# Projections as pairs of half-height matmuls, and a layer norm finished on transposed tiles

## The chip, the core and the metric

The kernel runs on one core of a Trainium2 chip. A core has a matrix engine (TensorE, in the profile PE, with its weight loads as PEld), three engines for elementwise work (VectorE, in the profile DVE; ScalarE, ACT; GpSimd, POOL) and an engine that issues most DMAs (SyncE, SP). TensorE reads its operands from SBUF and writes sums into eight banks of PSUM. Each engine works through its own queue in order; they wait for each other on semaphores. The metric is the time of one execution in microseconds (us) on the device.

## The reference

One sequence of 2048 rows of 448 numbers, bf16, goes through two blocks: linear attention with softmax features, and a gated MLP whose gate mixes the rows. `c` gives a shift, a scale and a gate for each block.

```
mod = (silu(c) @ w_mod)            # six vectors of 448: sa, ca, ga, sb, cb, gb
h = layernorm(x) * (1 + ca) + sa
q, k, v = h @ wqkv                 # 16 heads of 28
pq, pk = q @ w_phi, k @ w_phi      # per head
phi(p) = concat(softmax(p), softmax(-p))
o = (phi_q @ (phi_k.T @ v)) / (phi_q @ sum(phi_k) + 1e-6)
x = x + ga * (o @ wo)
h = layernorm(x) * (1 + cb) + sb
z = gelu(h @ w_in);  z1, z2 = halves of 896
g = w_sp @ layernorm(z2) + b_sp    # 2048 x 2048, over the rows
x = x + gb * ((z1 * g) @ w_out)
```

## The kernel before

The 2048 rows are 16 tiles of 128 rows. `fast_path` allocates everything by hand and then runs through a long string, `ORDER`: each word is a step with its arguments, a PSUM slot after `@` and an engine after `/`. The order of the words is the order of the instructions in each engine's queue. A branch at the end repeats the whole in a general form, `general_path`, if a softmax sum grew too large; it isn't taken here.

The stages, by the names of the steps:

- Start. `ld:...` are loads. `ct`, `ce` make silu(c); `csA`, `ccA` (line 757, `colform`) multiply it with the shift and scale parts of `w_mod`, as columns. `FT`, `ET`, `PF`, `EP` fold `w_phi` into the q and k weights. `du` are matmuls on zeros that keep TensorE busy meanwhile.
- First layer norm. `l1s` (830) takes the moments of a tile, `l1r` (838) raises to the power -1/2, `l1a` (841) writes the normalised tile into `xpad`, four blocks of 112 columns, each padded to 128. `T1` (846, by DMA) or `X` with `XE` (854, by TensorE) transposes it into `hT`, four blocks of 112 rows.
- Scale and shift of the norm are put into the weights. `SH` (775) and `SHw` (780) multiply the weights by a tile that holds the shift, which gives the weights one more row, the shift's product; `SC` and `SCw` (784, 786) multiply the weight rows by 1 + scale. In `hT` a padding column of ones meets that row, so the first block has 113 rows.
- The k stage. `kM` and `vM` (864, 872) project one tile to k and to v, four matmuls of 112 or 113 rows each. `kE`, `kF` (867) take both exponentials, `kS` (878) sums them on VectorE, `kR` and `kP` divide, `kA` (895) adds a tile's product of features and values into a sum over all tiles, 8 matmuls of 116 columns. `KV` (901) takes the sum out.
- The q/n stage. `qM` (912) makes q transposed, in groups of 512 rows and two blocks; `qE`, `qF` (917) the exponentials. `nM` (940) gives the numerators and sums of one tile, 8 matmuls of 120 columns. `nX`, `nC`, `nS` (944 to 953) make the normaliser, `nT` (956) and `nA` (962) apply it. `T2` (846) transposes by DMA. `wM`, `wN` (972, 970) project with `wo`; `wN` adds x by an identity matmul. `wR` (977, 979) evicts, `wQ` (984, 986) squares, `l2R` (992 to 995) and `l2r` (998) make the moments, `l2a` (1001) normalises, `T3` (1006) transposes into `hT`.
- The z/y stage, interleaved with the end of the one before. `zM` (1012) makes the half of z that is normalised, 8 matmuls a tile, `zG` its gelu, `zQ`, `zR`, `zW`, `zN` (1036) its layer norm. `yM` (1042) makes the other half transposed, 28 groups of four matmuls, `yG` (1045) its gelu. `tT` (1086) makes differences of z2 blocks for the next stage.
- The spatial stage. `gM` (1058) and `pM` (1109) multiply with `w_sp`, in part by a scheme of seven block products, `sS` (1098) makes its sums of weights; `oM` (1071) projects with `w_out`, `oE` (1074) adds x, `oD` stores. `W` (1050) loads `w_sp` by transposing DMAs, all on SP.

## Time and profile before

| what | us |
|---|---|
| three runs, median (lowest, highest) | 258.0 (256.01, 258.09) |
| the profiled execution | 257.26 |
| its span, first to last instruction | 255.4 |
| busy in the span: TensorE, VectorE, ScalarE, GpSimd | 243.3, 193.9, 116.9, 98.1 |

The page of a profile sums each engine's busy time. The windows give it by stretches of the span. The chain of waits starts at the last instruction and goes back, at each step to what released it; the matmuls' spacing can be read there. The groups of instructions give one line for each source line, operation and shape, with the number, the busy time and the mean duration of one in ns; after the second bar stand the idle time of the engine just before them and what ended most of it. A matmul's duration there includes its way through the array, so it's longer than the spacing of two in a row. The timeline gives single instructions with their start and length. L864 is line 864 of the kernel before.

### The profile page before, as it was taken

Reading aid. Unit: us, or ns where it says so; the run is one execution under the profiler, and the core shown is the slowest. Engines: PE = TensorE matmul, PEld = TensorE weight load, DVE = VectorE, ACT = ScalarE, POOL = GpSimd, SP = SyncE. Lnnn points to the kernel's source line nnn. Section 1 sums busy time; section 2 is a strip of 40 time slices with the busy share of each in tenths; the row PEclk is TensorE's granted clock in tenths of the full one; section 3 lists DMA queues with packets and bytes.
Section 4 is the critical chain, followed back from the end, with each engine's and each line's share of the span. In section 5 each row is a group of like instructions: output and inputs, shape, how many; then the busy total and the mean of one; then the engine's idle time right before and its main releaser. Section 6 shows DMA issues by size and latency. Waiting matters only on the chain.

```text
span 255.4 us, 4195 instructions
## 1 busy us (share of the span) xinstructions
PE 243.3 (95%) x1501; PEld 127.2 (50%) x1509; DVE 193.9 (76%) x417; ACT 116.9 (46%) x244; POOL 98.1 (38%) x115
## 2 busy tenths in 40 slices
...
PEclk9999999999999999999999999999999999999999
...
GB/s 176 263 296 125 163 235 247 292 18 0 82 130 166 200 52 76 82 180 112 67 16 0 136 189 6 0 3 41 181 106 5 55 90 0 0 3 3 16 78 61
DMA packets 68655, 25.22 MB, mean 99 GB/s; under 512 B 58129, under 2 KB 68498, under 8 KB 68626
## 3 DMA queue, kind: packets, MB, share of 16 engines
...
q14 instruction: 15, 0.12, 0.1%
...
## 4 chain that ended last, share of the span: by engine, by line
PE 81%; DMA 5%; ACT 4%; DVE 4%; issue 2%; POOL 1%; SPq 1%; DVEq 0%; POOLq 0%; ACTq 0%
PE f_psum L1109 28%; PE f_psum L1071 8%; PE f_psum L1012 8%; PE f_psum L1042 7%; PE f_psum L1058 5%; PE f_psum L864 5%; PE f_psum L872 4%; PE f_psum L912 3%; DMA f_hT<-f_xpad 3%; PE f_psum L972 3%; PE f_psum L895 3%; DMA f_oo<-f_oo 2%; PE f_psum L726 2%; PE f_psum L940 1%; DVE f_t L956 1%
## 5 line engine op out<-in xcount | busy, mean ns | idle before, releaser
L1109 PEld LDWEIGHTS <-f_z2n 128*128 128x128 bf16 x192 | 18.7, 98 | 22.4
L1012 PE MATMUL f_psum<-f_win,f_hT 112*128 112x448 bf16 (+1 forms) x128 | 26.3, 352 | 1.0 <-DMA f_hT<-f_xpad 1.0
L1109 PE MATMUL f_psum<-f_wsp,f_z2n 128*128 128x512 bf16 x119 | 27.2, 379 | 0.1
L1042 PE MATMUL f_psum<-f_hT,f_win 113*128 113x512 bf16 (+1 forms) x112 | 26.1, 378 | 0.2 <-ACT f_z1T L1045 0.2
L1109 PE MATMUL f_psum<-f_hT,f_Eq 128*128 128x512 bf16 x92 | 22.3, 379 | 0.2
L1071 PE MATMUL f_psum<-f_wout,f_z1T 128*128 128x448 bf16 x112 | 21.7, 352 | 0.0
L1129 ACT COPY f_Eq<-f_psum 128x512 f32<-128x512 f32 x4 | 2.3, 586 | 41.0 <-PE f_psum L1109 41.0
L1012 PEld LDWEIGHTS <-f_hT 112*128 112x128 bf16 (+1 forms) x128 | 12.2, 97 | 13.3 <-DMA f_hT<-f_xpad 1.9
L1045 ACT ACTIVATE f_z1T<-f_psum 128x512 bf16<-128x512 f32 x28 | 16.0, 597 | 4.5 <-PE f_psum L1042 4.4
L878 DVE TENSOR_REDUCE f_ksum<-f_E 128x32 f32<-128x896 bf16 x16 | 16.8, 1067 | 1.0 <-ACT f_E L867 0.9
L917 ACT ACTIVATE f_Eq<-f_psum 112x1024 bf16<-112x1024 f32 x16 | 16.0, 1035 | 2.7 <-PE f_psum L912 2.7
L1042 PEld LDWEIGHTS <-f_win 113*128 113x128 bf16 (+1 forms) x112 | 10.7, 97 | 12.7 <-issue 0.4
L1016 ACT ACTIVATE f_z2g<-f_psum 128x896 bf16<-128x896 f32 x16 | 14.6, 914 | 4.9 <-PE f_psum L1012 3.9
L956 DVE TENSOR_TENSOR f_t<-f_psum,f_w 128x896 bf16<-128x896 f32 x16 | 16.7, 1084 | 0.2
L867 ACT ACTIVATE f_E<-f_psum 128x448 bf16<-128x448 f32 x32 | 15.4, 555 | 1.8 <-PE f_psum L864 0.9
L1071 PEld LDWEIGHTS <-f_z1T 128*128 128x128 bf16 x112 | 10.9, 98 | 10.0
L972 PE MATMUL f_psum<-f_win,f_oo 112*128 112x448 bf16 x64 | 14.4, 353 | 1.4 <-DMA f_oo<-f_oo 1.3
L1109 PEld LDWEIGHTS <-f_Eq 128*128 128x128 bf16 x96 | 9.4, 98 | 11.3 <-issue 0.2
L998 POOL TENSOR_TENSOR f_v<-f_v,f_mhalf 128x2 f32<-128x2 f32 x8 | 7.2, 904 | 20.3 <-DVE f_v L995 20.3
L912 PE MATMUL f_psum<-f_hT,f_Wq 113*128 113x512 bf16 (+1 forms) x64 | 14.9, 378 | 0.0
L998 POOL TENSOR_TENSOR f_zv<-f_zv,f_mhalf 128x2 f32<-128x2 f32 x8 | 5.7, 717 | 22.0 <-DVE f_zv L995 22.0
L1074 DVE TENSOR_TENSOR f_xpad<-f_psum,f_x 128x448 bf16<-128x448 f32 x16 | 9.8, 619 | 5.8 <-PE f_psum L1071 5.8
...
## 6 DMA issues: line engine op xcount, KB each, us to landing
...
```

The costliest lines, as they stand in the source:

```text
L867: nc.scalar.activation(out=Er[i % NR][:, s, :], in_=ps["k" + str(i)][:, 0, 0:D], func=ACT.Exp, scale=1.0 - 2.0 * s)
L878: nc.vector.tensor_reduce(out=ksum[:, i], in_=Er[i % NR][:].rearrange("p s (c f h) -> p (s c) h f", c=4, h=HP), axis=AX.X, op=ALU.add)
L912: nc.tensor.matmul(t[:, u, :], lhsT=Wq[0:KR[m], m, cc * CB:cc * CB + P], rhs=hT[0:KR[m], 4 * st:4 * st + 4, m, :], start=(m == 0), stop=(m ...
L917: nc.scalar.activation(out=Eq[st // 2][0:CB, 2 * c2:2 * c2 + 2, s, (st % 2) * 512:(st % 2 + 1) * 512], in_=ps["q" + str(n)][0:CB, :, :], f ...
L956: nc.vector.tensor_tensor(out=tr[i % 2][:], in0=numv(i)[:, :, :, 0:DH], in1=wr[i // 2 % 2][:, i % 2].unsqueeze(3).to_broadcast([P, 2, H, D ...
L972: nc.tensor.matmul(t[:, 0, 0:D], lhsT=oT[0:CB, i % 4, cc, :], rhs=wo_s[0:CB, cc, :], start=(cc == 0 and not with_x), stop=(cc == KC - 1))
L1012: nc.tensor.matmul(t[:, hf, 0:D], lhsT=hT[0:KR[m], i, m, :], rhs=win_s[0:KR[m], m, FH + hf * D:FH + (hf + 1) * D], start=(m == 0), stop=(m ...
L1016: nc.scalar.activation(out=stage_b()["z2g"][i % NZ][:], in_=ps["z" + str(i)][:, :, 0:D], func=ACT.Gelu_apprx_tanh, accum_out=zs1[:, i:i + 1])
L1042: nc.tensor.matmul(t[:, 0, :], lhsT=win_s[0:KR[m], m, fc * P:(fc + 1) * P], rhs=hT[0:KR[m], 4 * st:4 * st + 4, m, :], start=(m == 0), stop ...
L1045: nc.scalar.activation(out=stage_b()["z1T"][:, fc, st * 512:(st + 1) * 512], in_=ps["y%d_%d" % (st, fc)][:, 0, :], func=ACT.Gelu_apprx_tanh)
L1071: nc.tensor.matmul(ps["o" + str(t)][:, 0, 0:D], lhsT=later["z1T"][:, fc, t * P:(t + 1) * P], rhs=wout_s[:, fc, :], start=(fc == 0), stop=( ...
L1109: nc.tensor.matmul(t[:, 0, :], lhsT=b[:, j, f * P:(f + 1) * P], rhs=a[:, j, :], start=(PSTART[k] and j == 0), stop=(j == NH - 1), skip_gro ...
```

## The change

Rows and tiles. The 448 rows of a projection's contraction were four blocks of 112. Now they lie as seven halves of 64 in four blocks of 128 rows that begin at rows 0, 128, 192 and 320; rows 192 to 255 lie in two blocks. The weights are loaded in that form (`load_half`, two DMAs for one), `l1a` and `l2a` write the normalised tile in it (`lap`), with no padding.

```diff
+    HB = 64
+    OV = 192
+    ROWS = [0, P, OV, OV + P]
...
+    def load_half(eng, dst, src):
+        for a in range(2):
+            eng.dma_start(out=dst[:, 2 * a:2 * a + 2], in_=src[a * OV:a * OV + 2 * P].rearrange("(k p) n -> p k n", p=P))
...
+    def lap(v):
+        return bass.AP(v.tensor, v.offset, [list(v.ap[0]), [OV, 2], [1, 2 * P]])
```

Pairs. `rows_pair` computes two outputs u = 0 and 1, in two banks. In a first phase u = 0 takes the lower halves of the four blocks and u = 1 the upper halves, in turns. A second phase takes the other halves: three for each output, without the doubled one. Between the phases an empty instruction on TensorE waits for the last matmul of the first phase; `ORDER` says when the second phase comes, by a step with a `b` at its end (`zM:0 ... zMb:0`).

```diff
+    def rows_pair(key, outs, lhs, rhs, second_rows=((0, 2, 3), (0, 1, 3)), n=4, start=True, stop=True, flip=0):
+        def go(seq, first, last):
+            for k, (u, h, m) in enumerate(seq):
+                ins = nc.tensor.matmul(outs(u, m), lhsT=lhs(u, h, m), rhs=rhs(u, h, m), start=(first and k < 2),
+                                       stop=(last and k >= len(seq) - 2), skip_group_check=True)
+                yield ins
+
+        one = list(go([(u, u ^ flip, m) for m in range(n) for u in range(2)], start, False))
+
+        def two():
+            mark = nc.tensor.nop()
+            tc.add_manual_dep(mark.ins, one[-1].ins.name, mybir.DependencyInfo(mybir.DependencyClass.Sync, mybir.DependencyReason.DATA), reason="row halves")
+            list(go([(u, 1 - u ^ flip, m[u]) for m in zip(*second_rows) for u in range(2)], False, stop))
+
+        second[key] = two
...
     def zM(i, slot):
         t = ps["z" + str(i)] = bank(slot, "z2_ps")
-        for hf in range(2):
-            for m in range(KC):
-                nc.tensor.matmul(t[:, hf, 0:D], lhsT=hT[0:KR[m], i, m, :], rhs=win_s[0:KR[m], m, FH + hf * D:FH + (hf + 1) * D],
-                                 start=(m == 0), stop=(m == KC - 1))
+        rows_pair("zM%d" % i, lambda u, m: t[:, u, 0:D], lambda u, h, m: hT[half(h), i, m, :],
+                  lambda u, h, m: win_s[half(h), m, FH + u * D:FH + (u + 1) * D])
```

Two outputs are: k and v of a tile (`kv`, for `kM` and `vM`), the two blocks of a `qM`, the two halves of a `zM`, two blocks of a `yM` (14 pairs for 28). `kA`, `nM` and `wM` are written as pairs too, with all 8 halves for each output, since their rows aren't shared (128 or 112 rows a block); `wM` now takes two tiles at a time. `yG` evicts two banks at once.

Scale and shift. `SH`, `SHw`, `SC`, `SCw` and their tiles are gone. Scale and shift stand as columns in `ca1`, `sa1`, `cb1`, `sb1` and are applied to the transposed tile: in the eviction `XE` where TensorE transposes (tiles 0 to 7, four more than before), and in place by `h1` (tiles 8 to 15) and `h2` (all, for the second norm) where a DMA does.

```diff
+    def affine(eng, out_, in_, sc, sh):
         if eng is nc.scalar:
-            nc.scalar.activation(out=out_, in_=in_, func=ACT.Copy, scale=sc)
+            nc.scalar.activation(out=out_, in_=in_, func=ACT.Identity, scale=sc, bias=sh)
         else:
-            eng.tensor_scalar(out=out_, in0=in_, scalar1=sc, scalar2=None, op0=ALU.mult)
+            eng.tensor_scalar(out=out_, in0=in_, scalar1=sc, scalar2=sh, op0=ALU.mult, op1=ALU.add)
...
+    def hS(a, b, m, eng, sc, sh):
+        v = hT[:, a:b, m, :]
+        affine(eng, v, v, sc[:, m:m + 1], sh[:, m:m + 1])
```

Smaller edits. For 13 tiles `kS` becomes `kH` (GpSimd adds the two halves of the features) and `kG` (VectorE sums the rest); 3 keep `kS`. `nX` takes out both normaliser columns, `nC` is gone, `nS` is split into `nS`, `nV`, `nW`, some on GpSimd. `l2R` and `zR` may run on GpSimd, with one instruction more. `guard2` is split in two. The matmuls on zeros (`du`) shrink from 35 to 17.

`ORDER` is written anew. What the prediction speaks of: the branch `hint` comes first, the table load for gelu (`gt`) at the start; loads leave ScalarE's queue for SP's but for two; `T1` runs four times for six; five of eight `qM` come before `KV` instead of three; 9 of 16 `tT` and 11 instead of 2 `zN` go to GpSimd; 12 `wR` instead of 7 and 8 `wQ` instead of 3 go to VectorE; `h1` has 6 steps on VectorE and 2 on ScalarE, `h2` 12 on VectorE, 13 on ScalarE and 7 on GpSimd; `guard` moves from the spatial to the z/y stage. One line of each:

```diff
-zQ:0/S nM:10@A1 l2a:5/G nA:8/V zG:1 nM:11@A0 T3:4,6 yM:0,6@B0 nA:9/V nX:11 nX:10 zQ:1/S nC:11 zM:2@A2 nC:10 nS:5 T2:8,10 yG:0,6 zR:0,2 wQ:6/S
...
+nMb:12 T3:2,4 l2r:4,6 nV:5 T2:8,10 nW:5/V nX:12 nT:10 nS:6/G l2R:6,8/G nV:6 zM:0@A0 nA:10/V nT:11 zMb:0 nW:6/G l2r:6,8 nT:12 zM:1@A1 zG:0 l2a:4/G
```

The spatial stage's `gM`, `pM` and `oM` stay as they are.

347 lines of the change are left out of this document (175 added, 172 removed).

## The prediction

> **What bounds the kernel now.** I read the page first, then the windows cut at the stage borders, then the chain of waits, then the groups of instructions, and last the timeline where two engines meet.
>
> ```profile
> span 255.4 us, 4195 instructions
> ...
> PE 243.3 (95%) x1501; PEld 127.2 (50%) x1509; DVE 193.9 (76%) x417; ACT 116.9 (46%) x244; POOL 98.1 (38%) x115
> ...
> PEclk9999999999999999999999999999999999999999
> ```
>
> The profiled execution took 257.26 us, its span is 255.4; the median of the three runs, 258.0, is 0.3% above it. TensorE's clock is full throughout, so durations can be compared across the span. The windows cut the span at the first k matmul (18.4), at the end of the k/v sums (56.4), at the first `zM` (81.2), at the first `gM` (142.7) and at the last output add (250.9).
>
> ```profile
> core 0: us, PE busy (x) PEld busy (x) DVE busy (x) ACT busy (x) POOL busy (x), PEclk, DMA share, GB/s
> 0.00:18.40 18.40, 16.05 (x171) 11.87 (x172) 13.21 (x42) 10.36 (x19) 7.61 (x29) 1.00 0.98 244
> 18.40:56.40 38.00, 37.92 (x303) 22.27 (x302) 35.98 (x71) 30.22 (x58) 20.94 (x24) 1.00 0.89 187
> 56.40:81.20 24.80, 21.51 (x177) 12.12 (x175) 19.14 (x54) 20.77 (x41) 15.17 (x14) 1.00 0.53 89
> 81.20:142.70 61.50, 60.02 (x333) 29.95 (x334) 49.05 (x147) 51.28 (x121) 23.16 (x26) 1.00 0.44 88
> 142.70:250.90 108.20, 107.78 (x523) 50.96 (x529) 75.90 (x106) 4.23 (x8) 31.18 (x23) 1.00 0.26 53
> ```
>
> Columns after the length are busy times. In the k stage (second row) TensorE is full and VectorE nearly so (36.0 of 38.0); in the q/n stage (third row) nobody is full, a chain of latencies sets it; in the z/y stage (fourth) TensorE has 60.0 of 61.5; the spatial stage (fifth) is TensorE alone, and the diff leaves its matmuls as they are.
>
> What one matmul costs on the path is its spacing in the chain of waits (start, length, what):
>
> ```profile
> 22.63 2.28 PE f_psum L864 x12
> ...
> 40.02 0.42 PE f_psum L895 x8
> ...
> 143.32 6.64 PE f_psum L1058 x30
> ```
>
> ```profile
> 57.18 0.38 PE f_psum L761 x16
> 57.56 0.86 PE f_psum L940 x16
> 58.42 1.51 PE f_psum L780 x8
> 59.94 3.47 PE f_psum L912 x16
> ...
> 77.37 3.77 DMA f_hT<-f_xpad
> 81.14 0.05 issue
> 81.19 1.69 PE f_psum L1012 x8
> ```
>
> 448 columns: 2.28/12 = 0.190 us; 512 columns: 3.47/16 = 0.217; the 116 and 120 columns of `kA` and `nM`: 0.053; one column with its weight load: 0.38/16 = 0.024. So weight loads hide entirely behind 52 ns of streaming, and the number of passes through the array is what counts.
>
> **The change, part by part.** *Passes.* A projection over 448 rows now takes four matmuls of 112 rows per output. In the new `rows_pair` two outputs take 14 matmuls of 64 rows, two at a time on different halves of the array and into different banks: 7 passes instead of 8, if two halves take the time of one matmul. That saves 16 x 0.190 = 3.0 us on k/v, 8 x 0.217 = 1.7 on q, 3.0 on z and 14 x 0.217 = 3.0 on y: 10.8. `kA`, `nM` and `wM` keep their number of passes (8 pairs for 8 matmuls): 0. The shift matmuls `SH` and `SHw` go: 28 x 0.19 = 5.3. Four more tiles are transposed on TensorE (16 x 0.05 = 0.9). TensorE thus loses 15.2 us of path work, none of it in the spatial stage.
>
> The trace has no matmul of 64 rows. The nearest rows bound a pair from both sides: two serial matmuls are 2.0 of one; nothing but a hidden second load and issue is 1.0, since 2 x 0.024 = 0.048 us of load and issue still fits into the smallest pass, 0.053. Below 1.0 is excluded, because the columns still have to stream. I take 1.0: it lies by the row of single columns, and every load in this trace is hidden.
>
> *The wait in the middle.* Each pair group has a second phase that must not start before the first has landed in the banks, and an empty instruction on TensorE waits for it; all matmuls behind it in TensorE's queue wait too.
>
> ```profile
> L1012 PE MATMUL f_psum<-f_win,f_hT 112*128 112x448 bf16 (+1 forms) x128 | 26.3, 352 | 1.0 <-DMA f_hT<-f_xpad 1.0
> ...
> L972 PE MATMUL f_psum<-f_win,f_oo 112*128 112x448 bf16 x64 | 14.4, 353 | 1.4 <-DMA f_oo<-f_oo 1.3
> ```
>
> A matmul is over 352 - 190 = 162 ns after the next could start. In the new ORDER 15 of the 94 second phases follow their first phase with no TensorE work between, most others have 0.2 to 1.5 us between: 15 x 0.162 = 2.4 us, about 0.8 of it in the z/y stage. The order also passes 16 times between half-height and full-height matmuls, nearly all in the k stage. No row shows such a passage; bounds are 0 and one drain, 16 x 0.162 = 2.6, taken as the upper one, but in a stage where VectorE sets the pace. The Trainium skill, TensorEngine Tiling (Array Packing), section Key Properties, says that changing the tiling mode drains TensorE, which speaks against this change; by it the upper bound holds, and the total is 249 if TensorE should set the pace there, 246 if VectorE does.
>
> *z/y stage.* TensorE's 60.0 are 48.6 for z and y, 6 `nM` (2.5) and 10 output projections (8.6). Afterwards: 42.5, 2 `nM` (0.8) and 8 projections (6.1), together 49.4; the rest is moved ahead, into a stage where TensorE stands idle for 3.3 us and loses 4 x 4 shift matmuls (3.0) and two q groups. So what is late next are the other engines.
>
> ```profile
> L1036 DVE TENSOR_SCALAR f_z2n<-f_z2g,f_zm,f_zv 128x896 bf16<-128x896 bf16 x14 | 8.8, 663 | 3.0 <-POOL f_zv L998 2.9
> ...
> L885 POOL TENSOR_TENSOR f_phik<-f_E,f_kr 128x896 bf16<-128x896 bf16 x4 | 7.1, 1779 | 9.1 <-DVE f_kr L882 5.1 <-PE f_psum L864 3.3 <-ACT f_Eq L917 0.7
> ...
> L962 POOL TENSOR_TENSOR f_oo<-f_t 128x448 bf16<-128x448 bf16 x5 | 5.2, 1046 | 2.5 <-DVE f_t L956 2.4
> ...
> L1086 DVE TENSOR_TENSOR f_Eq<-f_z2n 128x768 bf16<-128x768 bf16 x4 | 3.0, 756 | 0.0
> ...
> L1036 POOL TENSOR_SCALAR f_z2n<-f_z2g,f_zm,f_zv 128x896 bf16<-128x896 bf16 x2 | 2.4, 1204 | 0.2
> ```
>
> Nine `zN` and nine `tT` pass from VectorE to GpSimd. VectorE loses 9 x 0.66 + 9 x 0.65 = 11.8 (0.65 is a middle of the four `tT` groups; the one shown is the longest); the other moves (more `wR` and `wQ` on it, `h2` new, `nC` and most of the moments gone) roughly cancel: 49 - 12 = 37. GpSimd gains 9 x 1.20 = 10.8 and nine `tT` of 768 elements, between the 448 of 1.05 and the 896 of 1.78, say 1.55: 14. So 23 + 25 = 48. ScalarE's 51.3 falls, since 28 `yG` become 14 of double width and 5 `wR` and 5 `wQ` leave it, while 13 `h2` come.
>
> Now the price of that cover. When both run, they slow each other:
>
> ```profile
> 134.59 0.55 DVE L1086 TENSOR_TENSOR f_z2n<-f_z2n 128x768 bf16<-128x768 bf16 x1
> ...
> 137.10 4.62 POOL L929 TENSOR_TENSOR f_wout<-f_wout,f_g_rep 128x448 bf16<-128x448 bf16 x4
> 137.17 2.35 DVE L1036 TENSOR_SCALAR f_z2n<-f_z2g,f_zm,f_zv 128x896 bf16<-128x896 bf16 x2 [0.82 <-POOL f_zv L998]
> 139.44 1.38 DVE L1086 TENSOR_TENSOR f_Eq<-f_z2n 128x768 bf16<-128x768 bf16 x1
> ```
>
> Alone a `tT` takes 0.55, beside GpSimd 1.38; two `zN` 2.35. With GpSimd busy nearly all the stage, VectorE's 5 `zN` (+0.5 each), 7 `tT` (+0.8) and some 17 short affine steps (+0.3) add 13: 37 + 13 = 50. TensorE 49, VectorE 50, GpSimd 48: no stage can be shorter than 50, and where the stage before stood 1.5 above its fullest engine, three equal ones will wait for each other more; I take 3.5. The stage: 61.5 to 53.5, **-8**.
>
> *q/n stage.* Its chain runs from `nM` over the normaliser, the transposes and the second layer norm to `zM`, with 3.77 us for one DMA transpose. The change takes the shift and scale of `win` out (cover, not path), adds one affine step `h2` on the transposed tile and joins two tiles per `wM` (one more tile's 0.76). Bounds -2 and +2; I take **-0.5**.
>
> *k stage and start.* The path to the first k matmul loses `SH` and twelve weight scalings; its new path needs both modulation loads, whose tile landed at 10.6 (row below), then a scaled eviction `XE`. That frees up to 5 us.
>
> ```profile
> 10.57 0.47 PEld L761 LDWEIGHTS <-f_wm 112*128 112x128 bf16 x16 [0.17 <-DMA f_wm<-in_w_mod_dram]
> ...
> 18.45 0.92 PE L864 MATMUL f_psum<-f_Wk,f_hT 113*128 113x448 bf16 x4
> ```
>
> ```profile
> L878 DVE TENSOR_REDUCE f_ksum<-f_E 128x32 f32<-128x896 bf16 x16 | 16.8, 1067 | 1.0 <-ACT f_E L867 0.9
> ...
> L841 DVE TENSOR_SCALAR f_xpad<-f_x,f_nm,f_rs 128x448 bf16<-128x448 bf16 x4 | 1.5, 366 | 0.0
> ...
> L732 ACT ACT_TABLE_LOAD x1 | 1.3, 1283 | 0.0
> ```
>
> But VectorE, with 49.2 in the first two windows, sets the pace. It saves 13 of 16 `kS` (13.9) and gets 13 `kG` over half the elements (0.55 each, bounds 0.53 and 1.07: +7.2), eight more `l1a` (+2.9) and some sixteen affine steps of about 0.3 (+4.8, replacing 5 scalings): about -2 net, while GpSimd's 13 new half sums of 448 elements (1.05 or more each) run beside it. Most of the earlier start is eaten: **-2.5**, bounds -6 and +2.
>
> *Queues.* Loads of k, v, q and the two `win` halves become two DMAs each with 512 rows for 448; on SP, which also takes three loads over from ScalarE's queue, 17 load issues become 25, in front of the spatial weights' transposes, which have 60 us to spare. 0.17 MB more at 244 GB/s is 0.7 us of a full first window, inside the bound. `T1` falls from six to four. Moving the Gelu table load to the start takes 1.3 us of ScalarE out of the q/n stage, or puts as much in if it has to be loaded again. The branch hint moved to the front and `guard` moved ahead lie beside idle engines: 0; a late branch would lengthen the 4.5 us behind the last add.
>
> The sum: -8 - 0.5 - 2.5 = -11, **257.3 - 11 = 246 us**.
>
> **The rivals.** *The halves overlap only in part* (slower). Let a pair take f of a matmul. For it: no row shows one; against it: no load is exposed. The z/y stage's 49.4 reach the old 60.0 at f = 1.21, the point from which it decides. At f = 1.3 they are 64, the stage 67 (+6), the k stage gains 35.6 x 0.3 = 10.7 us of TensorE work and ends 3 later: **266**. Chance 0.09. The Trainium skill, TensorE: Matmul & The Clock Gate, section Measured speedup vs the span model, gives four row tiles at 3.07 times one; an estimate from that is f = 4/3.07 = 1.30. No run here shows it yet.
>
> *The halves don't overlap at all*, so the change doesn't do what it says: all 102 us of paired passes twice, some 10 of it in idle time: **338**. Chance 0.04.
>
> *GpSimd becomes the bound.* If its operations stretch too beside VectorE, 48 us of it become 58, the stage is as long as before, and the rest nets to -2: **255 to 258**. Chance 0.14. Against it: the four gate products above kept 4.62/4 = 1.15 each while VectorE paid. For it:
>
> ```profile
> 191.28 1.15 POOL L1132 TENSOR_TENSOR f_junk<-f_Eq,f_bsp 128x512 f32<-128x512 f32 x1
> ...
> 192.33 1.22 DVE L1098 TENSOR_TENSOR f_hT<-f_hT,f_win 128x2048 bf16<-128x2048 bf16 x1
> 192.51 2.05 POOL L1133 TENSOR_TENSOR f_Eq<-f_Eq,f_bsp 128x512 f32<-128x512 f32 x1
> ```
>
> Here GpSimd pays, 2.05 for 1.15, and VectorE keeps its time.
>
> *TensorE stays the bound throughout* and all 15 come back, with an earlier start: below 237. Chance 0.05.
>
> **How the numbers follow.** The forecast, 237 to 255, has 0.68. One per cent of 258 is what a measurement can tell from no change, so faster means below 255.4: 0.68 + 0.05 + 0.02 of the GpSimd case = 0.75; within: 0.12; slower: 0.13. The range 237 to 258 leaves out the two overlap rivals and the largest gain, 0.18; its lower end is the stage sums at their favourable bounds (50 for z/y, -2 for q/n, -6 for k), its upper end the GpSimd case.
>
> **What would show it.** In the new profile: first and last starts of z and y matmuls, spaced 0.095 and 0.109 per half on average (right) or 0.19 and 0.22 (no overlap); the z/y window near 53 with TensorE near 50 and GpSimd above 45; VectorE's `tT` above 1 us; `zM` starting about 24 us after the sums; the spatial window still 108. It is wrong if the z/y window keeps its 61 us, or if the spatial window changes.

## The result, and the profile after

The changed kernel took 297.43 us (median of four runs, 295.65 to 298.46) where the kernel before took 257.78 beside it: 1.154 times as long, 95% interval 1.148 to 1.161. The prediction was 246, within 237 to 258. An execution more than 1.5% above the fastest of its kernel (one each of e5, e7 and e16, and one of the kernel before) counts in the medians below, but not in the ratios.

The page of the profile after, the lines that answer to the three of before:

```profile
span 293.8 us, 5440 instructions
...
PE 250.4 (85%) x2114; PEld 126.2 (43%) x2122; DVE 220.7 (75%) x393; ACT 114.4 (39%) x220; POOL 157.3 (54%) x192
...
PEclk9577998999867697799999999995999999999998
```

VectorE has 27 us more to do, not less, GpSimd 59 more, and TensorE's clock is no longer full: its mean over the span is 0.914. To see where the time went, I cut both spans at five marks: the first exponential of k (`kE`), the last pair of steps of `KV`, the first `zG`, the first `gM`, the last `oE`. All stage lengths below are between the starts of these steps, in profiled executions, one of each kernel.

| kernel | to first `kE` | k stage | q/n | z/y | spatial | last `oE` |
|---|---|---|---|---|---|---|
| before | 19.9 | 36.6 | 26.5 | 59.9 | 108.0 | 250.9 |
| after | 18.5 | 62.5 | 37.1 | 55.0 | 116.2 | 289.3 |
| difference | -1.4 | +25.9 | +10.6 | -4.9 | +8.2 | +38.4 |

Only the start and the z/y stage are shorter, the latter by less than forecast; the other three stages lose 44.7 us. The windows of the changed kernel between these marks (columns as in the windows of before), and then the first of the kernel before:

```profile
0.00:81.00 81.00, 60.41 (x723) 33.76 (x723) 63.31 (x129) 46.93 (x85) 45.60 (x59) 0.87 0.66 151
81.00:118.10 37.10, 28.81 (x370) 15.80 (x372) 27.48 (x62) 16.78 (x42) 20.15 (x44) 0.76 0.53 93
118.10:173.10 55.00, 51.23 (x503) 25.25 (x499) 42.41 (x102) 45.52 (x87) 46.12 (x64) 0.98 0.38 64
173.10:289.40 116.30, 109.97 (x523) 51.36 (x529) 86.93 (x102) 5.17 (x8) 45.46 (x28) 0.97 0.25 49
```

```profile
0.00:56.50 56.50, 54.07 (x473) 34.21 (x474) 49.26 (x113) 40.58 (x76) 28.64 (x53) 1.00 0.92 205
```

Up to `KV` VectorE works 63.31 us for 49.26 and is idle 17.7 for 7.2: of the 24.5 us by which that mark is later, 14.0 are more VectorE work and 10.5 more waiting.

**The work.** These groups of instructions of the changed kernel answer to the rows of `kS`, `kP`, `l1a`, `zN` and the gate products of before:

```profile
L1067 POOL TENSOR_SCALAR f_z2n<-f_z2g,f_zm,f_zv 128x896 bf16<-128x896 bf16 x11 | 13.6, 1244 | 0.4
...
L904 DVE TENSOR_REDUCE f_ksum<-f_hs 128x32 f32<-128x448 f32 x13 | 12.0, 932 | 3.9 <-POOL f_hs L901 3.9
...
L911 DVE TENSOR_TENSOR f_phik<-f_E,f_kr 128x896 bf16<-128x896 bf16 x9 | 9.5, 1054 | 0.6
...
L1137 DVE TENSOR_TENSOR f_hT<-f_Eq 128x2048 bf16<-128x2048 bf16 x4 | 8.0, 2026 | 0.0
...
L859 DVE TENSOR_SCALAR f_xpad<-f_x,f_nm,f_rs 128x512 bf16<-128x512 bf16 x12 | 6.2, 536 | 2.1 <-POOL f_rs L856 2.1
...
L948 DVE TENSOR_TENSOR f_wout<-f_wout,f_g_rep 128x448 bf16<-128x448 bf16 x5 | 5.8, 1215 | 0.0
...
L1067 DVE TENSOR_SCALAR f_z2n<-f_z2g,f_zm,f_zv 128x896 bf16<-128x896 bf16 x5 | 5.5, 1122 | 4.0 <-POOL f_zv L1031 4.0
```

A `kG` takes 932 ns over half the elements; the whole `kS` of before took 1067. So the 13 split sums save VectorE 13.9 - 12.0 = 1.9 us. And steps that the diff leaves as they are have become slower on VectorE, where GpSimd now runs much more beside it. `kP` and a sum of `sS` in the groups of the kernel before:

```profile
L885 DVE TENSOR_TENSOR f_phik<-f_E,f_kr 128x896 bf16<-128x896 bf16 x12 | 7.2, 625 | 0.1
...
L1098 DVE TENSOR_TENSOR f_hT<-f_Eq 128x2048 bf16<-128x2048 bf16 x4 | 5.2, 1290 | 0.0
```

So `kP` takes 1054 ns for 625, the sum 2026 for 1290, and `zN` 1122 for the 663 of the prediction's row. A gate product takes 1215; before, VectorE had one on `wout`, at 383, and one on `wo`, at 909, too few to say by how much it slowed. Single instructions point to GpSimd: in the kernel before most sums take 1.22 us while GpSimd is idle, and the two that start at 152.81 and 154.91, beside it, 2.18; in the changed kernel the `kP` at 59.90 takes 0.63 with GpSimd idle and the one at 70.67 1.97 beside a `kP` of GpSimd's. Not every step beside it pays: the `kP` at 42.53 keeps its 0.61.

**The waiting.** The chain of waits of the changed kernel shows one turn of its k stage, then the last steps ahead of `KV` (start, length, what):

```profile
49.00 7.29 PE f_psum L799 x85
...
57.37 1.04 POOL f_hs L901
58.43 0.96 DVE f_ksum L904
59.42 0.36 DVE f_kr L908
59.90 0.64 DVE f_phik L911
...
70.67 1.98 DVE f_phik L911
...
73.93 5.77 DVE f_wout L948 x5
```

Where a sum was one step on one engine, it now passes GpSimd and comes back. And five gate products, which have nothing to do with the k stage, stand on VectorE directly ahead of `KV`, for which the `nM` of the next stage wait. They take 5.77 us, of which about 2 hold `KV` up: the last `kA` ends at 77.5, and before that `KV` could not have begun. The 7.29 us of TensorE on the chain are the projections of late tiles in one lump, because their transposes came late. In the timeline SyncE's issues, then the last moments of tiles 8 to 11 on VectorE and their powers on GpSimd:

```profile
19.08 5.49 SPq L1089 DMA_TRANSPOSE f_wsp<-in_B_w_sp_dram  x3
38.54 10.35 SPq L864 DMA_TRANSPOSE f_hT<-f_xpad  x4
```

```profile
35.26 0.18 DVE L845 BATCH_NORM_AGGREGATE f_mv<-f_st 128x2 f32<-128x6 f32 x1
```

```profile
36.47 1.04 POOL L856 TENSOR_TENSOR f_rs<-f_rs,f_mhalf 128x4 f32<-128x4 f32 x1
```

SyncE issues nothing from 24.6 to 38.5, since `T1` of tiles 8 to 15 needs powers that GpSimd computes at 36.5 and 39.1. Two queues made them late: VectorE takes the last moments that the first of them needs at 35.3, behind its `kG`, `l1a` and `XE`, and a `kP` holds GpSimd until 35.9. In the kernel before the first `T1` is issued at 22.1 us.

### The profile page after: what moved, and what is told of

Its sections match the earlier page's. It is cut to its first block, busy times and chain, and to the rows that moved or that the text cites. A ratio compares the mean times of both kernels' runs of the same rounds, so it can differ in the third digit from the quotient of the medians.

```text
span 293.8 us, 5440 instructions
## 1 busy us (share of the span) xinstructions
PE 250.4 (85%) x2114; PEld 126.2 (43%) x2122; DVE 220.7 (75%) x393; ACT 114.4 (39%) x220; POOL 157.3 (54%) x192
## 4 chain that ended last, share of the span: by engine, by line
PE 45%; DVE 25%; POOL 13%; issue 7%; ACT 4%; DMA 4%; SPq 0%; DVEq 0%; POOLq 0%; ACTq 0%
PE f_psum L1148 21%; PE f_psum L799 13%; PE f_psum L1110 7%; DVE f_ksum L904 3%; POOL f_z2n L1067 3%; DMA f_hT<-f_xpad 3%; DVE f_hT L1137 3%; PE f_psum L1097 2%; DVE f_wout L948 2%; POOL f_zv L1031 2%; DVE f_phik L911 2%; DVE f_hT L785 2%; DVE f_Eq L1137 1%; POOL f_hs L901 1%; DMA f_x<-in_A_x_dram 1%
## 5 line engine op out<-in xcount | busy, mean ns | idle before, releaser
L799 PEld LDWEIGHTS <-f_hT 64*128 64x128 bf16 x448 | 22.2, 102 | 36.9 <-DVE f_hT L785 8.4
L799 PE MATMUL f_psum<-f_Wk,f_hT 64*128 64x448 bf16 x112 | 30.1, 403 | 5.5 <-DVE f_hT L785 3.0
L799 PE MATMUL f_psum<-f_win,f_hT 64*128 64x448 bf16 x224 | 27.5, 377 | 6.2 <-DMA f_hT<-f_xpad 2.6
L799 PE MATMUL f_psum<-f_wv,f_hT 64*128 64x448 bf16 x112 | 30.1, 403 | 0.0
L799 PE MATMUL f_psum<-f_hT,f_win 64*128 64x512 bf16 x196 | 23.4, 376 | 0.1
L901 POOL TENSOR_TENSOR f_hs<-f_E 128x448 f32<-128x448 bf16 x13 | 13.9, 1072 | 16.0 <-ACT f_E L891 10.7
L1148 PE MATMUL f_psum<-f_hT,f_Eq 128*128 128x512 bf16 x92 | 22.3, 379 | 0.2
L799 PE MATMUL f_psum<-f_win,f_oo 64*128 64x448 bf16 (+1 forms) x128 | 16.2, 376 | 3.1 <-DVE f_t L979 2.9
L799 PE MATMUL f_psum<-f_hT,f_Wq 64*128 64x512 bf16 x112 | 18.0, 453 | 0.1
L799 PE MATMUL f_psum<-f_vaug,f_phik 64*128 64x116 bf16 x256 | 12.5, 223 | 6.4 <-DVE f_phik L911 6.3
L1148 PE MATMUL f_psum<-f_Eq,f_oo 128*128 128x512 bf16 x47 | 13.0, 421 | 5.1 <-DVE f_z2g L1175 4.9
L1110 PEld LDWEIGHTS <-f_z1T 128*128 128x128 bf16 x112 | 10.9, 98 | 10.0
```

Of the source, the lines that this page charges most:

```text
L799: ins = nc.tensor.matmul(outs(u, m), lhsT=lhs(u, h, m), rhs=rhs(u, h, m), start=(first and k < 2), stop=(last and k >= len(seq) - 2), skip ...
L901: nc.gpsimd.tensor_tensor(out=hsum[i % 2][:], in0=ev[:, :, 0:DH // 2], in1=ev[:, :, DH // 2:DH], op=ALU.add)
L1110: nc.tensor.matmul(ps["o" + str(t)][:, 0, 0:D], lhsT=later["z1T"][:, fc, t * P:(t + 1) * P], rhs=wout_s[:, fc, :], start=(fc == 0), stop=( ...
L1148: nc.tensor.matmul(t[:, 0, :], lhsT=b[:, j, f * P:(f + 1) * P], rhs=a[:, j, :], start=(PSTART[k] and j == 0), stop=(j == NH - 1), skip_gro ...
```

## The experiments

Each kernel starts from the one named. All are judged beside runs of the kernel before on the same chip; "against after" gives the difference of the medians, and in brackets that of the ratios times 258 us.

| run | median | ratio to before (95%) | against after |
|---|---|---|---|
| e1 | 303.44 | 1.174 (1.170, 1.178) | +6.0 (+5.1) |
| e17 | 294.46 | 1.144 (1.136, 1.152) | -3.0 (-2.7) |
| e2 | 290.66 | 1.121 (1.117, 1.126) | -6.8 (-8.5) |
| e3 | 294.0, one execution | | -3.4 |
| e4 | 290.75 | 1.123 (1.117, 1.129) | -6.7 (-8.1) |
| e7 | 284.25 | 1.096 (1.091, 1.102) | -13.2 (-15.0) |
| e8 | 275.56 | 1.068 (1.060, 1.076) | -21.9 (-22.3) |
| e10 | 263.37 | 1.016 (1.010, 1.022) | -34.1 (-35.6) |
| e12 | 296.09 | 1.144 (1.137, 1.152) | -1.3 (-2.6) |
| e14 | 262.23 | 1.017 (1.011, 1.022) | |
| e15 | 258.86 | 1.004 (1.000, 1.007) | |
| e5 | 258.14 | 0.997 (0.993, 1.000) | |
| e6 | 269.06 | 1.040 (1.035, 1.045) | |
| e16 | 259.41 | 1.003 (0.999, 1.007) | |
| e9 | 259.66 | 1.007 (1.003, 1.011) | |
| e11 | 256.11 | 0.989 (0.987, 0.992) | |
| e18 | 258.48 | 1.001 (0.998, 1.003) | |
| e13 | 255.23 | 0.987 (0.984, 0.991) | |

### What are the halves worth?

**e1**: the changed kernel with its order, but each pair group as matmuls one after the other: for each output the blocks with all their rows, of the third block, which holds 64 rows twice, only the other 64.

```diff
+        proj = second_rows == ((0, 2, 3), (0, 1, 3))
+        for u in range(2):
+            for m in range(n):
+                h = 1 if proj and m == 2 else None
...
-            mark = nc.tensor.nop()
...
+            pass
```

> The changed kernel with every pair undone: the same ORDER, engines and row layout, but each output takes four full-height matmuls in one phase (128, 128, 64 and 128 rows for a projection), and nothing in the second. Theory A (the half-height pairs are good, and the time went to VectorE, GpSimd and the chains between them): TensorE's path work grows by about 11 us, most of it in its idle time, so 297 to 305 us, and no stage gets shorter by more than 2 us. Theory B (the pairs, their phase wait or the passage between heights cost the time): the k stage, 68 us now, falls by 10 us or more, and the time goes below 285.

**e5** and **e6** ask the same without the change's order. e5 is the kernel before up to `KV`, and behind it the second half of the change: `win` in halves, `h2`, pairs in `zM` and `yM`, in an order of my own. e6 is e5 with those pairs undone as in e1.

```diff
-    def SHw(n, slot):
...
+    def h2(a, b, m, eng):
+        hS(a, b, m, eng, cb1, sb1)
...
+        rows_pair("zM%d" % i, lambda u, m: t[:, u, 0:D], lambda u, h, m: hT[half(h), i, m, :],
+                  lambda u, h, m: win_s[half(h), m, FH + u * D:FH + (u + 1) * D])
```

> The kernel before with one half of the change alone: scale and shift of the second layer-norm on its transposed tiles (32 steps of 128x256 behind T3) and z and y as pairs of 64-row matmuls over seven halves; the projections of k, v, q, n and w, the first layer-norm, the single sums and the order up to the last k tile stay as before; the steps between KV and the spatial stage stand in an order of their own. Theory A (the halves are worth 6 us in the z/y stage and the 32 steps fit beside TensorE; the loss of the whole change is in its first half): 5 to 8 us under the kernel before, 250 to 253 us, from the first gelu of z to the first gM 52 to 55 us, k stage and spatial stage as before (36 and 108 us). Rival B (the 32 steps and the gelu pieces are a new bound on VectorE and ScalarE, so the second half gives nothing by itself either): 257 us or more.

> The kernel of e5 with its pairs undone: each unit of z and y in four matmuls (three of 128 rows, one of 64), everything else and the order the same. Theory A (TensorE bounds this stage, a pair costs one matmul): 16 x 2 x 0.19/2 us for z and 28 x 0.215/2 us for y, 6 us more than e5 where all of it is on the path, at least 4. Rival B (something else bounds it): within 1.5 us of e5. Rival C (the order alone is the gain): both e5 and e6 are under the kernel before by more than 4 us.

e6 is 10.9 us slower than e5, more than the 6 us of passes that the pairs of z and y save. e1 is 6.0 slower than the change; its z/y stage is 11.7 longer, but its spatial stage, against its expectation, 6.0 shorter. The z/y window of e6 says that TensorE is full, and its chain of waits why:

```profile
87.10:154.30 67.20, 66.63 (x289) 22.20 (x290) 54.13 (x145) 48.08 (x92) 40.73 (x44) 1.00 0.47 83
```

```profile
93.85 0.97 PE f_psum L828 x4
94.82 0.76 PE f_psum L1010 x4
```

Four matmuls of one `zM` output take 0.97 us, four of a `wM` 0.76. The undone form passes from 128 rows to 64 and back in each output, and that costs 0.21. So these two runs compared the halves with something slower than what there was before. **e16** takes the passages out of e6, **e17** out of e1 for z and y alone (its k, v and q keep them), and **e18** is e11 (below) in the form of e16: all four blocks with 128 rows, so that 64 rows count twice and z is another z.

```diff
-                h = 1 if proj and m == 2 else None
+                h = None
```

> e6 with one thing changed: the third block of each z and y projection is also taken with all 128 rows, so that no 64-row matmul stands among the 128-row ones any more. The number of matmuls stays (four for an output); the 64 rows that lie in two blocks are counted twice, so z is another z. In the chain of waits of e6 a wM of four 112-row matmuls takes 0.76 us, eight zM matmuls (two outputs) take 1.93 to 2.01 and sixteen yM matmuls 4.08, where four times 0.190 and 0.217 would give 1.52 and 3.47. Theory A: each passage between 128 and 64 rows, two for an output, costs some 0.08 to 0.10 us of TensorE; e6 holds 60 outputs and so about 11 us of it, and the 10.9 us between e6 and e5 priced more than the halves. Then eight zM matmuls take 1.52, TensorE in the z/y stage falls from 66.6 to 56, the stage from 67.2 to 58, the time to 259 to 262, and the halves are worth 1 to 4 us. Theory B: the matmuls are slow for another reason (128 rows instead of 112, the rows' place), and nothing changes: eight zM matmuls still 1.9 to 2.0, 267.5 to 270.5 us.

> e1 with the same change for zM and yM alone: their third block with all 128 rows, the rows that lie in two blocks counted twice; k, v and q as in e1. Theory A (a passage between 128 and 64 rows costs 0.08 to 0.10 us): the z/y stage falls from 66.7 to 57 to 59, the spatial stage gets some of the 6 us back that it had won, the time is 296 to 300. Theory B (no price on the passage): 302 to 305, z/y stage 66 to 67.

> e11, the fastest kernel so far, with its pairs undone as in e16: four matmuls of 128 rows for each output of z and y, the 64 rows that lie in two blocks counted twice, so z is another z. In e11 the z/y stage takes 53.4 us with TensorE busy 51.85; eight matmuls for seven are 32 x 0.095 + 28 x 0.109 = 6.1 us more of TensorE. Theory A (TensorE bounds the stage; the halves are worth what they save): z/y 58 to 60, 260 to 263 us. Theory B (as in e16, where TensorE had 54.9 of 58.0 and the time was 1.3 above e5: the chain through GpSimd and the transposes bounds the stage as much, and the pairs pay for passages and for the wait in their middle): z/y 54 to 56, 256 to 258.5 us, the halves are worth 0 to 2.5.

The z/y window of e16:

```profile
84.90:144.20 59.30, 55.79 (x291) 26.89 (x291) 51.97 (x138) 47.28 (x92) 42.27 (x45) 1.00 0.56 94
```

TensorE has 10.8 us less than in e6 with as many matmuls: 60 outputs with two passages each, 0.09 us a passage. Theory A of the passages held for e16, and e17 went even below its range: with full height in z and y and the order of the change the time is 294.5 us, with halves 297.4; the intervals of the ratios overlap, so that the halves are worth nothing there that can be measured. In the better orders they are worth 1.3 us by the medians and 1.7 by the ratios, whose intervals just touch (e16 against e5), and 2.4 or 2.9 (e18 against e11, by theory B of that run: TensorE isn't the only bound).

This isn't for want of overlap. TensorE's timeline in the changed kernel, at full clock:

```profile
60.81 0.35 PE L799 MATMUL f_psum<-f_wv,f_hT 64*128 64x448 bf16 x1
60.81 0.35 PE L799 MATMUL f_psum<-f_Wk,f_hT 64*128 64x448 bf16 x1
```

```profile
163.64 2.83 PE L799 MATMUL f_psum<-f_win,f_hT 64*128 64x448 bf16 x28
166.29 6.87 PE L799 MATMUL f_psum<-f_hT,f_win 64*128 64x512 bf16 x62
```

Two halves start together, and 14 pairs take 166.29 - 163.64 = 2.65 us, 0.189 each, the time of one full matmul: f = 1.0, and the rivals that rested on f are out. What the empty instruction costs can be read too, where a second phase follows its first at once:

```profile
121.58 1.73 PE L799 MATMUL f_psum<-f_win,f_hT 64*128 64x448 bf16 x14
123.14 1.92 PE L799 MATMUL f_psum<-f_hT,f_win 64*128 64x512 bf16 x14
```

The seven pairs of one `zM` take 123.14 - 121.58 = 1.56 us where 7 x 0.189 is 1.32: 0.24 for the wait between the phases. In the row of 14 pairs, two tiles whose phases take turns, there is none.

That the halves gain nothing is for want of a stage that TensorE alone bounds. The chain of waits of the changed kernel from 118 to 175 us, summed by line:

```profile
by line: POOL f_z2n L1067 16.3%; issue 12.8%; POOL f_zv L1031 9.7%; PE f_psum L799 7.1%; DVE f_xpad L1034 5.7%; POOL f_v L1031 4.3%; DVE f_z2n L1067 3.9%; POOL f_z2n L1125 3.5%; POOL f_oo L1125 2.9%; DVE f_x L1008 2.9%; POOL f_Eq L1125 2.8%
```

It runs through GpSimd's `zN`, powers and `tT`; matmuls have 7% of it. With full height (e17) TensorE is busy 54.41 of 55.7 us, with halves 51.23 of 55.0: less work for TensorE only uncovers that chain. Both are near to full, and taking the steps off GpSimd (e4, below) shortens the stage by no more than 1.9.

**e9** and **e11** are e5 in two other orders behind `KV`, since e5 had lost in the q/n stage (32.9 us for 26.5) what it gained in z/y (55.1 for 59.9). Its timeline, and the window in which that begins:

```profile
64.12 1.78 PE L973 MATMUL f_psum<-f_KVbd,f_Eq 112*128 112x120 bf16 x16 [2.17 <-DVE f_t L989]
```

```profile
64.00:68.00 4.00, 3.88 (x37) 2.76 (x38) 3.26 (x10) 0.37 (x2) 1.03 (x1) 0.51 0.34 64
```

TensorE waits 2.17 us for VectorE, and the granted clock (third number from the end) is then 0.51, in the next 4 us 0.63. That a wait is paid twice in this way is not a rule: e16, in the same order, waits as long at the same place,

```profile
64.61 1.01 PE L978 MATMUL f_psum<-f_KVbd,f_Eq 112*128 112x120 bf16 x16 [2.16 <-DVE f_t L994]
```

and its clock stays at 1.00. Its q/n stage takes 28.6 us, so that some 4 of the 6 us that e5's profiled execution lost there went with the clock.

```diff
-h2:0,1,0/V nS:5 ld:win0/Y nA:8/G
+l2a:2/G wQ:4/S ld:win0/Y h2:0,1,0/S T2:6,8
```

```diff
-l2a:2/G wQ:4/S ld:win0/Y h2:0,1,0/S T2:6,8
+kP:15/V gr:0@A1 ld:win0/Y kA:15@A0 KV:1
```

> The second half of the change alone, as e5, in an order whose stretch from KV to the first z leaves TensorE no wait above 1.2 us (in e5 a wait of 2.17 us ended at 64.12 us and the granted clock was 0.51 in the 4 us after it). Theory A (e5 lost to that wait what its z/y stage of 55.1 us had won against 59.9): q/n stage 27 to 29 us (e5 32.9, before 26.5), z/y 53 to 56, 251 to 254 us. Rival B (the steps of scale and shift lengthen the way to the first z by themselves): q/n again 31 us or more, 257 us or more.

> The second half of the change alone, as e5 and e9, in an order that also keeps the loads of win ahead of the transposes T2 that it would hold up (in e9 a T2 issued at 81.68 us, 1.2 us behind the load of win0, held TensorE for 3.21 us). Theory A (the halves and the 32 steps are a gain of 4 us or more once the stretch from KV to the first z has no such wait): q/n 27 to 29 us, z/y 53 to 55, 251 to 254 us. Rival B (the stretch to the first z is longer by the steps themselves): q/n 31 us or more and 256 us or more.

e9 has no such wait at that place, and its clock is full there, but by its numbers it came out as rival B (q/n stage 32.3 us). It lost 3.2 us at a place that the timeline shows, SyncE's first and then TensorE's:

```profile
80.44 1.08 SPq L663 DMA_DIRECT2D f_win<-in_B_w_in_dram  x2
81.68 1.24 SPq L879 DMA_TRANSPOSE f_oo<-f_oo  x1
```

```profile
87.44 1.69 PE L1005 MATMUL f_psum<-f_win,f_oo 112*128 112x448 bf16 x8 [3.21 <-DMA f_oo<-f_oo]
```

The transpose `T2` is issued behind two loads of `win` (448 KB each) and lands 5.7 us later; the median of its kind in that run is 3.1. In e11 that load stands ahead of `KV`. e11 is the fastest kernel of this study with the whole computation, 1.1% faster than the kernel before (interval 0.8 to 1.3); and as e18, its twin at full height, is at 1.001, the gain is that of the halves. It missed the time of theory A too and meets both conditions of rival B. That the steps `h2` are the reason, as B says, isn't shown: without them (e13) the stage still takes 31.1 us. Its q/n stage, 32.5 us, is nearly full on VectorE from 64 to 89 us, as one window out of it shows,

```profile
68.00:72.00 4.00, 2.80 (x30) 1.82 (x28) 3.90 (x7) 2.51 (x7) 2.94 (x3) 1.00 0.16 33
```

and in its z/y stage TensorE's timeline has the passages again, as e11 keeps its output projections `wM` at full height:

```profile
111.42 0.93 PE L1005 MATMUL f_psum<-f_win,f_oo 112*128 112x448 bf16 x4
112.29 1.69 PE L818 MATMUL f_psum<-f_hT,f_win 64*128 64x512 bf16 x14
113.90 0.93 PE L1005 MATMUL f_psum<-f_win,f_oo 112*128 112x448 bf16 x4
```

The four `wM` matmuls take 112.29 - 111.42 = 0.87 us where 4 x 0.190 is 0.76, the seven pairs 1.61 where 7 x 0.217 is 1.52: 0.1 a passage. The change writes `kA`, `nM` and `wM` as pairs too, though that saves no pass; it saves passages.

### Do scale and shift on the tiles cost?

**e13** is e11 without its 36 `h2`; **e14** is e10 (below) without its 12 `h1`, **e15** without those and its 32 `h2`.

```diff
-h2:0,1,0/V nS:5 ld:win0/Y
+nS:5 ld:win0/Y
```

> The kernel of e11 without its 32 steps h2: scale and shift of the second layer-norm are left out of the result, everything else stands as it was. Theory A (the steps behind T3 are the price that the second half pays: they lie between each transpose and its z, and their 15 us of engine time lie on engines that are busy): 3 to 6 us under e11, from KV to the first z 2 to 4 us shorter. Rival B (they are hidden; the stretch from KV to the first z is set by VectorE's steps on the numerators): within 1.5 us of e11.

> The kernel of e10 without its 12 steps h1: scale and shift of the first layer-norm are left out for tiles 4 to 15, everything else the same. Theory A (of the 10 us that the k stage of e10 is longer than before's 36.6, these steps in the path of the transposed tiles are a third or more): k stage 43.5 us or less, 3 us or more under e10. Rival B (they are hidden, the k stage is set by what stands in VectorE's and ScalarE's queues: moments, sums, exponentials): within 1.5 us of e10.

> The kernel of e10 without h1 (tiles 4 to 15) and without the 32 steps h2, both left out of the result. Theory A (the steps of scale and shift on tiles are what the change pays with): e10 less what e14 and e13 give together, at least 6 us, so 257 us or less, under the kernel before. Rival B: less than 3 us under e10.

Leaving out `h2` in e11 gives 0.9 us (0.5 by the ratios), leaving out `h1` in e10 1.1, which by the ratios is nothing, so both runs went by rival B; both left out of e10 give 4.5 by the medians and 3.3 by the ratios. So `h2` is nearly covered in e11, and `h1` in e10; in e10 the two together are worth some 3 us. `h2` alone was not left out of e10.

### What does the order cost?

**e2**: `kS` for all tiles, no `kH` and `kG`. **e3**: the half sums in bf16 instead of f32. **e4**: `tT`, `zN`, the moments' steps and `h2` from GpSimd to VectorE, the order kept.

```diff
-kH:0 kE:1 kv:2@A1 l1s:8 W:0,2 kH:1 kv:3@C kG:1
+kE:1 kv:2@A1 l1s:8 W:0,2 kv:3@C kS:1/V
```

```diff
-    hsum = [aph.tile([P, 8, DH // 2, HP], F32, name=f"f_hs{r}") for r in range(2)]
+    hsum = [aph.tile([P, 8, DH // 2, HP], BF, name=f"f_hs{r}") for r in range(2)]
```

```diff
-zN:1/G
+zN:1/V
...
-tT:1,0,2/G
+tT:1,0,2/V
...
-zR:0,2/G
+zR:0,2/V
```

> The changed kernel with the feature sums of all 16 tiles in one VectorE step again (kS for kH and kG). VectorE's step goes from 0.93 to 1.07 us, 13 x 0.14 = 1.8 us more, and GpSimd loses 13.9 us and a link of the chain from exponential to division. Theory A1 (the split is one of the main losses): the k stage, 68 us, falls by 5 us or more, time 285 to 293. Theory A2 (it is only VectorE's amount of work): the k stage grows by about 2 us, 297 to 300. Theory B: no change.

> The changed kernel with the half sums kept in bf16, which rounds them once more. If VectorE's sum over them (0.93 us for 448 numbers in f32, against 1.07 for 896 in bf16) is slow because of the f32 input, it falls to 0.5 to 0.6 us, and the k stage by 3 to 5 us; if it is slow because of GpSimd beside it or of the stride, it stays above 0.85 and the time at 297.

> The changed kernel with the steps of the z/y stage that went to GpSimd back on VectorE, in the same places of ORDER: tT, zN, l2R, zR, nS, nW, h2. Theory A (the two engines slow each other, so what moves to GpSimd is paid twice): VectorE's tT falls from 1.9 to 0.6 us and its zN from 1.12 to 0.52, the sS of the spatial stage from 2.0 to 1.3, GpSimd has 50 us less; the z/y stage (65 us) stays between 60 and 66, TensorE's gap of 8 us at the head of the spatial stage goes, and the time falls by 5 to 12 us, 285 to 292. Theory C (VectorE's amount of work alone): the z/y stage grows by 10 us or more, above 305.

Undoing the split sums (e2) gains 6.8 us, 4.7 of it in the k stage, though VectorE then sums all the elements again; with the `kH` gone from GpSimd, a `kP` on VectorE takes 855 ns on average for 1054. e3, a single execution, shows why the split saved VectorE so little; its group:

```profile
L904 DVE TENSOR_REDUCE f_ksum<-f_hs 128x32 f32<-128x448 bf16 x13 | 7.7, 602 | 3.9 <-POOL f_hs L901 3.9
```

The same sum over the same 448 elements takes 602 ns from bf16 and 932 from f32. In e4 the spatial stage is shorter by 5.7 us and the z/y stage by 1.9, while the k and q/n stages of that execution are 1.1 and 1.5 longer. Its groups, and the sum over its windows up to the last `oE`:

```profile
L1064 DVE TENSOR_SCALAR f_z2n<-f_z2g,f_zm,f_zv 128x896 bf16<-128x896 bf16 x16 | 8.3, 537 | 1.5 <-POOL f_zv L1028 1.4
...
L1134 DVE TENSOR_TENSOR f_hT<-f_Eq 128x2048 bf16<-128x2048 bf16 x4 | 5.4, 1375 | 0.2 <-DMA f_Eq<-in_B_w_sp_dram 0.2
```

```profile
sum 284.50, PE 250.40 PEld 126.10 DVE 218.66 ACT 114.88 POOL 103.05; mean PE 62.60 PEld 31.53 DVE 54.67 ACT 28.72 POOL 25.76
```

GpSimd loses 54 us of work (157.3 to 103.1), VectorE gets all of it and is busy no longer than before the move (220.1 to 218.7): what the moved steps cost it, the steps beside them give back. All 16 `zN` take 8.3 us, where 5 took 5.5 beside GpSimd.

**e7**: e2 and e4 together, and the gate products on `wout` (`wts`) behind `KV` on GpSimd.

```diff
-wts:4/V
...
+wts:4/G
```

> The changed kernel with three groups of steps moved, nothing else: the sums of k in one step each on VectorE (as e2), tT, zN, l2R, zR, nS, nW and h2 from GpSimd to VectorE (as e4), and the seven gatings of wout from before KV to GpSimd behind the gelus of z. Theory A (each move takes its own time off the path; five gatings stood on VectorE from 73.93 to 79.70 us, 2 us of it after the last k tile's sum was in): 6.8 + 6.7 + 2 us under the changed kernel, 280 to 283 us, k stage 54 to 57 us. Rival B (the moves free the same idle time, another chain is late next): 285 us or more. Theory C (moved steps are most of the loss): 270 us or less.

It gains 13.2 us by the medians and 15.0 by the ratios, between the two theories: the three moves don't quite add up (8.5 and 8.1 by the ratios for the first two alone), and most of the 40 us are elsewhere.

**e8** keeps every function of the change (half-height pairs for all projections, `h1`, `h2`) and takes an order of my own: `kS` on VectorE, the moments and `T1` early, `wts` behind `KV`, six `T1` as in the kernel before, the spatial stage as before. **e10** is e8 with its `T1` ahead of the loads that had stood in front of them, one load of `wq` for two, and 26 more matmuls on zeros at the start; many other steps change places with these.

```diff
-kE:5 kP:3/V ld:win0/Y T1:8,10 kv:6@A2
+kA:1@A0 kS:3/V kAb:1 T1:8,10 kv:5@A1
```

> All of the change's functions (seven row halves for k, v, q, n, w, z and y, scale and shift on the transposed tiles), but from the first k tile to the spatial stage in another order and with another split of the engines: the sums of k in one step each on VectorE, the moments and the transposes T1 of tiles 4 to 15 ahead of the sums in GpSimd's and SP's queues, wout gated behind KV on GpSimd, 8 of 12 h1 and 19 of 32 h2 on GpSimd, tT and zR on VectorE; the spatial stage as in the kernel before. Theory A (the change's loss is its order and its split of the engines, not what it computes): k stage 42 to 46 us (after 62.5, before 36.6), q/n 25 to 30, z/y 54 to 57, spatial 108 to 110, in all 256 to 266 us. Rival B (the halves and the scale and shift in the path of every tile cost this time in any order): 280 us or more. In between: both.

> As e8 (all functions of the change, own order), with the transposes T1 and T2 ahead of the weight loads on SP (in e8 a T1 issued at 46.18 us behind win landed 6.7 us later and every engine stood for 4.5 us), wq loaded once (e8 loads it twice), and 26 dummy matmuls where TensorE waits before the first k tiles (the granted clock of the changed kernel is 0.50 from 8 to 18 us). Theory A (what is left of the loss in e8 is order too): k stage 43 to 48 us (e8 54.4), q/n 25 to 29, z/y 54 to 59, 257 to 265 us. Rival B (the k stage pays for the halves and the scale and shift in any order): k stage 50 us or more, 268 us or more.

e8 came out between the theories, and its timeline shows a loss of its own, SyncE's line and ScalarE's:

```profile
46.18 1.32 SPq L860 DMA_TRANSPOSE f_hT<-f_xpad  x1
```

```profile
52.90 0.81 ACT L779 ACTIVATE f_hT<-f_hT,f_sa,f_ca 128x512 bf16<-128x512 bf16 x1 [4.45 <-DMA f_hT<-f_xpad]
```

A `T1` issued behind two loads of `win` and one of `w_mod` lands 6.7 us later, and ScalarE, GpSimd and VectorE stand still for 4.5. With that mended, e10 takes 263.37 us: the order and the division among the engines, with one to three us for the matmuls on zeros (e12 below), are 34 of the 40 us. Its window up to `KV`:

```profile
0.00:62.50 62.50, 54.38 (x739) 32.18 (x741) 52.56 (x108) 43.91 (x81) 39.22 (x57) 1.00 0.83 191
```

VectorE's 52.56 are 3.3 above the kernel before, and `KV` ends 6.0 later. Without scale and shift (e15) it still ends at 60.8, 4.3 later; what the other 4 us are stays open. The z/y stage of e10, 57.1, is 2.8 shorter than before, q/n 3.0 longer.

**e12**: the changed kernel with only the 26 added matmuls on zeros of e10.

```diff
-l1a:1/V ce:2 X:1,1@1 ce:3
+l1a:1/V ce:2 du:18@6 X:1,1@1 ce:3
```

> The changed kernel in its own order with 26 more dummy matmuls, 18 ahead of the second tile's transposes (TensorE waits there from 6.6 to 8.6 us) and 8 ahead of the first k tile. Theory A (the granted clock of 0.50 from 8 to 18 us delays the first k tiles, and the delay runs through the k stage): clock 0.9 or more from 8 to 18 us, first exponential 1 us earlier, 2 to 4 us under the changed kernel, 293.5 to 295.5 us. Rival B (the k stage waits for its normalised tiles anyway): within 1 us of the changed kernel.

Windows of the start, of the changed kernel and of e12:

```profile
16.00:18.00 2.00, 2.00 (x14) 0.88 (x12) 1.39 (x5) 0.00 (x0) 0.54 (x1) 0.50 0.93 155
```

```profile
8.00:18.00 10.00, 8.07 (x109) 5.25 (x106) 7.33 (x25) 4.58 (x12) 1.58 (x3) 1.00 1.23 263
```

The clock from 8 to 18 us is mended, 0.50 to 1.00 (from 18 to 24 it is 0.72 in e12), and the first exponential comes 1.8 us earlier. The k stage gives 0.7 of that back, the spatial stage, where nothing was changed, 1.5, and the total, 1.3 us by the medians and 2.6 by the ratios, lies within the intervals. So the clock at the start is at most a small part of the loss.

## Why the prediction was wrong

**Pairs at f = 1.0: right.** 0.189 us a pair in an unbroken row of them, no load or issue exposed. That was argued from the rows of single columns, and it held.

**Empty instructions and passages.** A passage costs 0.09 to 0.11 us (e6 against e16, the timeline of e11), between the bounds 0 and 0.162; the change's 16 come to some 1.6 us. The Trainium skill, TensorEngine Tiling (Array Packing), section Key Properties, gives the drain without a price; the traces agree with it. It speaks not against the change, which stays at 64 rows for long stretches, but against using pairs here and there. An empty instruction with no work between its phases costs 0.24 us for the 0.162 of the sum. Both are far too small to explain 40 us.

**z/y stage, -8: the right way, but too large, and the reason mostly wrong.** It is 4.9 us shorter (3.4 by the prediction's own mark, the first `zM`: 58.1 for 61.5), with TensorE at 51.2 (forecast 49), GpSimd at 46.1 (48) and VectorE at 42.4 (50). VectorE came out lower because only two of its seven `tT` took 1.9 us beside GpSimd and five kept 0.55. But e17 at full height has 55.7: of the 4.9 only 0.7 are the halves', the rest is work moved ahead of the first `zG`, into a stage that became longer. What the halves take off TensorE leaves the chain through GpSimd.

**k stage and start, -2.5: the step that failed.** It came out at +24.5, far beyond its bounds of -6 and +2. The first term was VectorE's net of about -2. Its listed parts give less: -13.9 + 7.2 + 2.9 + 4.8 is +1.0, and the five scalings that go took 1.6, so -0.6; some casts, a copy and a memset that went too and that it didn't list, 1.9 together, make up the rest. By the groups above, `kG` took 12.0 for 7.2 (+4.8); `l1a` rose by 6.2 - 1.5 = 4.7 for 2.9 (+1.8); `kP` rose by 9.5 - 7.2 = 2.3 though three fewer ran there, and five gate products came in ahead of `KV` with 5.8, where one of 0.9 had stood (+4.9): neither was in the sum. The affine steps took 7.1 for 4.8 (+2.3; 3.6 for six `h1`, 3.5 for ten `XE`). With the -2 that is +14.1; measured are +14.0. Of the five gate products about 2 us held up `KV`. The row that should have warned is in the prediction: `tT` at 0.55 alone and 1.38 beside GpSimd. Its price was applied to the z/y stage; in the k stage the 13 `kH` were said to run beside VectorE and priced at nothing. The Trainium skill, GPSIMD Engine Reference, section Specifications, says that GpSimd shares its interfaces to SBUF with VectorE, in contention with VectorE instructions that have two SBUF inputs or run in a 2-port performance mode. The trace agrees in part: `kP` and the sums have two such inputs and slowed (1054 ns for 625, 2026 for 1290); `zN` slowed with one tensor as input, and whether it runs in such a mode no run here shows.

**The queues, counted at 0: the step that failed beside it.** The other 10.5 us up to `KV` are waits of VectorE that the sum had no term for. The prediction counted issues and bytes, and took it that fewer `T1` cost nothing; it didn't ask what stands ahead of each step in its engine's queue. The trace shows three places: `kG` waiting for `kH` (3.9 us in the group above), the moments and powers of eight tiles late behind other work on VectorE and GpSimd, the gate products ahead of `KV`. e7 prices three moves at 13.2 us (15.0 by the ratios), e10 order and division among the engines at 34 (35.6). How the other 21 divide was not tried one by one and stays open.

**q/n stage, -0.5: wrong, +10.6.** It was read as a chain of latencies that TensorE's savings would leave alone. In the changed kernel VectorE is busy 27.5 us there, longer than the whole stage was, and the clock is at 0.76; the first z matmul starts 34 us after `KV`, where 24 were expected. The Gelu table was loaded again at 114.8, the case that the prediction left open; ScalarE then still waited 2.0 us for TensorE, so that it cost nothing there. In e11, without the change's order, the stage is still 6.0 longer, VectorE nearly full. What each of these steps adds was not tried.

**Spatial stage unchanged: wrong, +8.2.** None of its matmuls changed. Its sums on VectorE went from 1290 to 2026 ns beside GpSimd (45.5 us busy there for 31.2), and TensorE had to wait for a VectorE step behind them:

```profile
201.66 3.57 PE L1148 MATMUL f_psum<-f_Eq,f_oo 128*128 128x512 bf16 x8 [4.95 <-DVE f_z2g L1175]
```

The windows around it give a granted clock of 0.78, 0.50 and 0.87 from 197 to 209 us, and TensorE is 2.4 us longer busy in the stage than before. This wait, another of 0.84 for a sum and the 2.4 make up the 8.2. In e4 TensorE's waits there shrink to 2.0, its busy time is 108.0 again, and 5.7 of the 8.2 come back.

**Clock full throughout: wrong.** It is 0.914, and 0.50 to 0.51 from 8 to 18 us, where the matmuls on zeros were cut from 35 to 17. At the start this is worth 1.3 us by the medians and 2.6 by the ratios, within the noise (e12); the drop in the spatial stage follows the wait of 4.95.

**The start, "most eaten": right.** The first exponential is 1.4 us earlier, and all of it is eaten.

**Scale and shift on the tiles**, costed as cover and a few VectorE steps: some 3 us together (e15 against e10).

**The rivals.** The slower forecasts rested on f. "GpSimd becomes the bound" named the right engine, at 255 to 258; it left out that GpSimd, full nowhere over a whole stage, would slow VectorE and hold others up through its queue outside the z/y stage too.
